# The current-token term of an RWKV layer moved from TensorE to VectorE, with a new written-out order

## The chip, the cores and the metric

One core of one Trainium2 chip. The metric is the device time of one execution, in microseconds (us), a median over several. One execution of each kernel was also taken by the hardware profiler; its rows are the source of every duration below. Engines: PE is TensorE (its weight loads are listed apart as PEld), DVE is VectorE, ACT is ScalarE, POOL is GpSimd, SP is SyncE, which here only issues DMAs.

## The reference

Four batches, eight heads, 768 tokens, head size 48. First an RWKV attention with a decaying state, then a channel MLP on the concatenated heads (384 channels), all in float32:

```python
for t in range(S):                       # attention, per batch and head
    y[t]  = r[t] @ (state + outer(u * k[t], v[t]))
    state = w[:, None] * state + outer(k[t], v[t])

x  = y, heads side by side               # [4, 768, 384]
xn = (x - mean(x)) / sqrt(var(x) + 1e-6) * g_ln
out = x + maximum(xn @ w_ch1, 0) @ w_ch2 # 384 -> 1536 -> 384
```

The part of `y[t]` that uses the token's own key and value is, per head, the scalar `sum_d r[t,d] * u[d] * k[t,d]` times the vector `v[t]`. This is the current-token term.

## The kernel before, in words

**Tiling.** The 3072 tokens are 24 chunks of 128, six chunks per batch. A chunk is a tile of 128 tokens by 384 channels. Step names, which the plan uses, stand in capitals with the chunk number.

**Attention of a chunk.** LK, LR, LV load k, r, v (192 KB each, SP queue). SK and SR multiply k and r by powers of w that depend on the row (tables Fk and Fr), in bfloat16, into `sck` and `scr`. CV casts v into `vv`. TR turns `scr` and `sck` on TensorE into `trs` (TC, or TCr and TCk, copy them out of PSUM); from chunk 14 on TKD turns k, and from chunk 20 on TRD turns r, by DMA instead. AT multiplies the turned tiles, 128 by 128 scores per head; AM (line 365) masks them into `A`. S (lines 382 to 402) adds k^T v into the state's PSUM tile, ZU and ZD turn that into the next state `Z`, Y (lines 428 and 436) gives the attention output from `Z` and `A`. In chunks 1 to 4 (`ZPE`) S also adds the last state into PSUM with one matmul (line 393).

**Current-token term.** Q multiplies the two halves of `trs` element by element (bfloat16, 128x512), on DVE or POOL. In S, four matmuls (line 386) multiply Q by `uwI`, two columns per head pair that hold u*w, so that eight columns of the PSUM tile get the per-head scalars. (r and k carry powers of w whose product leaves 1/w, hence u*w.) CC copies the eight columns out of PSUM into `cc` on ACT or DVE; VB (line 418, POOL) multiplies v by them; X (line 443, DVE) adds this to Y's output.

**MLP.** SQ gives the variance sum, XN the centred activations, RS the scale (POOL). LT and XT turn `xn` on TensorE, or LTD by DMA. UP (line 499) multiplies by the first weight matrix, RL (line 515 or 517) applies the maximum with zero, DN (line 527) multiplies by the second matrix, OT (line 583) scales and adds x, STO stores. `GROUPS` says how many chunks one UP handles, one or two. The first weights come as three blocks of 768 KB (LW1), are multiplied by -g and cast by SW; the second come by three casting DMAs from POOL's queue (IW2).

**Start.** w, as one row, is loaded (WF), its logarithm taken (LN) and spread over 128 rows by one float32 matmul (WBM, line 269); FK and FR make the tables. u and w are also loaded with channels on partitions (ROWSI: four DMAs of 4-byte elements on ACT's queue), as is g (LG, on SP). WL makes the decay of the state `WLZ`, UW makes `uwI`. WU and DU are dummy matmuls on a tile of zeros.

**What sets the order.** Nothing is scheduled at run time. `PLAN` is one list of steps with an engine letter (v, s, g for DVE, ACT, POOL); every engine and DMA queue runs its steps in the order of that list and waits at the head of its own queue. Buffers are rings (`SLOTS`).

Of the kernel before, what the change touches and what calls it, by code (L numbers as in the profile page):

```python
# [13 lines left out]
GROUPS = [1, 1, 1, 1, 1, 1, 1, 1, 2, 2, 2, 2, 2, 2, 1, 1, 1, 1]  # L14
ZPE = [1, 2, 3, 4]
K_BY_DMA = [14, 15, 16, 17, 18, 19, 20, 21, 22, 23]
SLOTS = {'kf': 10, 'rf': 10, 'vf': 10, 'sck': 3, 'scr': 3, 'vv': 4, 'trs': 3, 'q': 2, 'A': 2, 'cc': 4, 'Z': 3, 'ZS': 2, 'Vb': 3, 'x': 13, 'xn': 3, 'xT': 4, 'hT': 4, 'ot': 3}
PLAN = """
MW,0,v WF,0,- TL,0,s MI,0,g WU,13,- MM,0,g MP,0,v LN,0,s LG,0,- ROWSI,0,s WBM,0,- LR,0,-
UGC,0,s FK,0,s LK,0,- FR,0,s LR,1,- SR,0,g WL,0,s SK,0,v LK,1,- UW,0,g DU,24,- TR,0,-  # L20
SR,1,v LK,2,- TCk,0,v SK,1,v LV,0,- TCr,0,v SK,2,v DU,12,- AT,0,- LR,2,- TR,1,- CV,0,s
AMa,0,v LV,1,- Q,0,g AMb,0,v SR,2,v LW1,0,- DU,7,- Y,0,- S,0,- TCk,1,v CC,0,s TCr,1,v
CV,1,s ZU,0,v Q,1,g DU,10,- TR,2,- LV,2,- TC,2,v DU,4,- AT,1,- VB,0,g S,1,- SW,2,s
AMa,1,v LW1,1,- SW,1,g SW,0,s X,0,v Q,2,v CV,2,g XN,0,s AMb,1,v DU,20,- LT,0,- CC,1,v
SQ,0,s Y,1,- ZU,1,v LK,3,- VB,1,g AT,2,- XT,0,v SW,5,s SW,4,v RS,0,g UP,0,- LR,3,-
X,1,v SW,3,s AM,2,v S,2,- SK,3,g XN,1,s LW1,2,- UP,1,- RL,0,s SR,3,v LT,1,- IW2,0,g
SQ,1,s Y,2,- XT,1,v IW2,1,g RL,1,s CC,2,v DU,1,- TR,3,- ZU,2,v VB,2,g UP,17,- LV,3,-
TC,3,s SW,8,g UP,16,- X,2,v RL,17,s SW,7,v IW2,2,g AT,3,- SW,6,v RL,16,s CV,3,g Q,3,v
DU,3,- UP,18,- SQ,2,s XN,2,g UP,2,- AM,3,v RS,2,g RL,18,s LT,2,- DN,0,- RS,1,g XT,2,v
S,3,- RL,2,s UP,34,- CC,3,v VB,3,g Y,3,- RL,34,s ZU,3,v UP,32,- DN,1,- X,3,v UP,33,-  # L30
XN,3,v SQ,3,s LK,4,- RL,32,v LT,3,- DN,2,- RL,33,s XT,3,v RS,3,g LR,6,- UP,48,- SK,4,g
OT,0,v UP,50,- LR,4,- DN,4,- SR,6,v RL,50,s LK,5,- DN,5,- RL,48,s SR,4,v STO,0,- DN,6,-
LK,6,- SK,5,v TR,4,- OT,1,v UP,49,- LR,5,- DN,8,- RL,49,s SK,6,g LV,4,- DN,9,- TC,4,s
SR,5,v DN,10,- LK,10,- Q,4,v TR,5,- CV,4,s OT,2,v AT,4,- LV,5,- TC,5,s S,4,- AM,4,v
DN,12,- LV,7,- CC,4,s TR,6,- VB,4,g ZU,4,v Y,4,- LK,7,- Q,5,v AT,5,- TC,6,s CV,5,g
X,4,v DN,13,- LR,7,- AM,5,v SQ,4,s XN,4,g DN,14,- LV,6,- S,5,- LT,4,- SK,7,v Y,5,-
CC,5,s XT,4,s SR,7,v AT,6,- LR,8,- Q,6,v UP,64,- OT,3,v VB,5,g STO,2,- UP,65,- RL,64,s
AM,6,v LR,9,- TR,7,- RL,65,s UP,66,- LV,10,- X,5,v RS,4,g DN,16,- TC,7,v XN,5,s LK,8,-
SR,8,g DN,17,- SR,9,v RL,66,s CV,6,s LT,5,- LK,9,- AT,7,- SQ,5,s S,6,- Q,7,v DN,18,-
SK,8,g XT,5,s AM,7,v LK,17,- CV,7,s UP,82,- RS,5,g STO,3,- CC,6,s TR,8,- RL,82,s ZU,6,v  # L40
STO,1,- Y,6,- VB,6,g UP,80,- TC,8,v LV,9,- CV,10,s S,7,- X,6,v Q,8,g RL,80,s AT,8,-
LR,14,- XN,6,s Y,7,- OT,4,v UP,81,- CV,9,s SK,9,g AM,8,v LK,11,- DN,20,- RL,81,s SK,10,g
LT,6,- LR,13,- CC,7,v DN,21,- ZU,7,v SQ,6,s XT,6,v VB,7,g DN,22,- LR,10,- UP,96,- ZD,7,g
OT,5,v LV,8,- TR,9,- X,7,v RL,96,s RS,6,g UP,98,- LR,11,- TC,9,v XN,7,s SR,10,g UP,97,-
RL,98,s LR,17,- DN,24,- SQ,7,s Q,9,v SR,11,g CV,8,s LT,7,- STO,4,- AT,9,- XT,7,v RL,97,s
S,8,- LV,13,- TR,10,- UP,112,- SK,11,v CC,8,s TC,10,s LV,11,- ZU,8,v Y,8,- VB,8,g DN,25,-
RL,112,s LR,21,- Q,10,v ZD,8,g UP,114,- X,8,v LK,19,- AM,9,v S,9,- CV,11,g DN,26,- SQ,8,s
LV,14,- TR,11,- XN,8,v CC,9,s OT,6,v VB,9,g Y,9,- TC,11,s LR,12,- AT,10,- ZU,9,v DN,28,-
X,9,v ZD,9,g RL,114,s LK,13,- AM,10,v LT,8,- S,10,- CV,13,s UP,113,- RS,7,g XN,9,s LK,12,-
# [43 lines left out]
def kernel(  # L93
# [170 lines left out]
    def LN(i, e):  # L264
        nc.scalar.activation(out=ln_row[:], in_=w_row[:], func=ACT.Ln)
# [365 lines left out]
```

## Time and profile before

| | us |
|---|---|
| median of six runs | 157.02 |
| lowest and highest of them | 154.81, 158.37 |
| the profiled execution | 155.87 |
| its span in the profile | 154.1 |
| busy: PE, DVE, ACT, POOL | 143.2, 106.2, 88.5, 88.4 |
| MB moved by DMA | 25.53 |

The busy times are shares of one span: PE works during 93% of it, the other engines during 57% to 69%. The granted TensorE clock is 1.00 throughout. Matmul durations of the groups overlap one another, since the ends of matmuls are modelled; how long TensorE really needs for a run of matmuls is read from the chain of work that ended last, or from the distance between starts. So 12 UP matmuls of 128 columns take 0.67 us in an unbroken run, 4 DN matmuls 0.65 us.

### The profile page before, as it was taken

What the parts mean: (1) busy time and instruction counts of PE and PEld (TensorE: products, weight loads), DVE (VectorE), ACT (ScalarE), POOL (GpSimd) and SP (SyncE); (2) the same over time, 40 slices, a digit from 0 to 9 for tenths busy, and PEclk for the clock granted to TensorE, in tenths of its full rate; (3) what the DMA queues carried; (4) which work ended last, traced back from release to release, by engine and by line L of the source; (5) the groups of instructions that cost most, each with busy time, mean ns of one, the idle gap of its engine ahead of it and who ended that gap; (6) DMA issues with size and microseconds to landing.
All of it is one profiled execution on the core that took longest, in us unless ns stands there. A gap on an engine that the chain in (4) does not pass through costs nothing.

```text
span 154.1 us, 4643 instructions
## 1 busy us (share of the span) xinstructions
PE 143.2 (93%) x1866; PEld 115.2 (75%) x1866; DVE 106.2 (69%) x220; ACT 88.5 (57%) x190; POOL 88.4 (57%) x126
## 2 busy tenths in 40 slices
PE   7989597999999999899999999989999999899991
PEld 4877485877786788689678679768787877668880
DVE  2499687655998686978884979895977554555121
ACT  4512895436648658668878559437578345144440
POOL 3535888422575987487931999483734968531100
PEclk9999999999999999999999999999999999999999
DMA  3999899959989899989997989678353663212211
GB/s 50 207 213 359 165 309 208 226 117 216 222 187 240 166 210 203 204 173 197 227 212 146 260 151 220 134 172 152 99 138 79 90 195 98 68 51 78 80 51 51
DMA packets 93142, 25.53 MB, mean 166 GB/s; under 512 B 88385, under 2 KB 91586, under 8 KB 93122
## 3 DMA queue, kind: packets, MB, share of 16 engines
q1 hardware_dynamic: 91858, 24.06, 70.8%
q0 software_dynamic: 432, 1.18, 3.9%
q8 instruction: 14, 0.23, 0.7%
q10 hardware_dynamic: 832, 0.00, 0.3%
q14 instruction: 6, 0.05, 0.1%
HBM read 18.88 MB, written 4.72 MB: 153 GB/s over the span
## 4 chain that ended last, share of the span: by engine, by line
PE 40%; DMA 22%; POOL 10%; DVE 10%; SPq 9%; issue 4%; ACT 2%; DVEq 0%; POOLq 0%
PE o L527 17%; PE hp L499 16%; DMA kf<-in_k_dram 5%; DMA w_sb<-in_moe_w_ch_dram 4%; DMA w_f<-in_moe_w_ch_dram 4%; DVE A L365 4%; DMA xT<-xn 4%; SPq L317 3%; POOL Vb L418 3%; SPq L320 2%; DMA rf<-in_r_dram 2%; SPq L475 2%; POOL sck L201 2%; DMA vf<-in_v_dram 2%; PE at L355 2%
## 5 line engine op out<-in xcount | busy, mean ns | idle before, releaser
L515 ACT ACTIVATE hT<-hp 128x512 bf16<-128x512 f32 x70 | 41.2, 596 | 33.1 <-PE hp L499 32.2
L499 PE MATMUL hp<-xT,w_sb 128*128 128x128 bf16 (+1 forms) x648 | 57.0, 237 | 1.8 <-DMA xT<-xn 1.1
L527 PE MATMUL o<-w_sb,hT 128*128 128x384 bf16 x276 | 53.9, 326 | 1.6 <-DVE ot L583 1.0
L499 PEld LDWEIGHTS <-w_sb 128*128 128x128 bf16 x648 | 48.9, 114 | 6.0 <-DMA xT<-xn 1.6
L527 PEld LDWEIGHTS <-hT 128*128 128x128 bf16 x276 | 24.7, 98 | 13.8 <-issue 1.1
L365 DVE TENSOR_TENSOR A<-at,mask 128x1024 bf16<-128x1024 f32 (+1 forms) x26 | 29.4, 1135 | 0.9 <-PE at L355 0.7
L418 POOL TENSOR_TENSOR Vb<-vf,cc 128x384 f32<-128x384 f32 x24 | 20.2, 841 | 11.8 <-ACT cc L196 7.9
L583 DVE SCALAR_TENSOR_TENSOR ot<-o,rs,x 128x384 f32<-128x384 f32 x23 | 14.1, 614 | 17.0 <-PE o L527 15.7
L450 ACT ACTIVATE sqj<-x,sm 128x384 bf16<-128x384 f32 x24 | 14.7, 612 | 4.4 <-DVE x L443 4.3
L443 DVE SCALAR_TENSOR_TENSOR x<-y,Vb 128x384 f32<-128x384 f32 x24 | 13.3, 552 | 4.3 <-POOL Vb L418 2.8
L201 POOL TENSOR_TENSOR scr<-rf,Fr 128x384 bf16<-128x384 f32 x9 | 9.7, 1081 | 10.0 <-DMA rf<-in_r_dram 6.5
L201 POOL TENSOR_TENSOR sck<-kf,Fk 128x384 bf16<-128x384 f32 x10 | 10.3, 1040 | 8.6 <-DMA kf<-in_k_dram 6.1
L201 POOL TENSOR_TENSOR q<-trs 128x512 bf16<-128x512 bf16 x9 | 10.9, 1208 | 5.9 <-DVE trs L198 3.4
L201 POOL TENSOR_TENSOR Z<-ZS,WLZ 128x384 bf16<-128x384 f32 x12 | 12.2, 1014 | 2.3 <-DVE ZS L412 2.3
L201 DVE TENSOR_TENSOR sck<-kf,Fk 128x384 bf16<-128x384 f32 x14 | 8.6, 619 | 5.6 <-DMA kf<-in_k_dram 5.0
L196 ACT COPY trs<-tr 128x1024 bf16<-128x1024 bf16 (+1 forms) x12 | 10.4, 865 | 3.1 <-PE tr L336 3.1
L467 POOL TENSOR_TENSOR rs<-rs,expo 128x1 f32<-128x1 f32 (+1 forms) x18 | 11.1, 617 | 1.5
L201 DVE TENSOR_TENSOR q<-trs 128x512 bf16<-128x512 bf16 x15 | 8.1, 539 | 4.7 <-ACT trs L196 3.1
L196 ACT CAST vv<-vf 128x384 bf16<-128x384 f32 x16 | 8.2, 510 | 3.9 <-DMA vf<-in_v_dram 1.9
L201 DVE TENSOR_TENSOR scr<-rf,Fr 128x384 bf16<-128x384 f32 x15 | 9.1, 615 | 1.8 <-DMA rf<-in_r_dram 1.7
L259 PE MATMUL o<-warm 128*128 128x128 bf16 x94 | 9.1, 265 | 1.0 <-DVE warm L224 1.0
L355 PE MATMUL at<-trs 48*128 48x128 bf16 x192 | 9.5, 218 | 0.4 <-DVE trs L198 0.2
(72 smaller groups left out, 176.7 us busy)
## 6 DMA issues: line engine op xcount, KB each, us to landing
rf<-in_r_dram SPq DMA_DIRECT2D x24, 192.0 KB, 3.8
kf<-in_k_dram SPq DMA_DIRECT2D x24, 192.0 KB, 4.1
vf<-in_v_dram SPq DMA_DIRECT2D x24, 192.0 KB, 3.8
out_dram<-ot SPq DMA_DIRECT2D x23, 192.0 KB, 2.9
w_f<-in_moe_w_ch_dram SPq DMA_DIRECT2D x3, 768.0 KB, 6.7
w_sb<-in_moe_w_ch_dram POOLq DMA_DIRECT2D x3, 384.0 KB, 7.3
out_dram<-ot SPq DMA_DIRECT2D x2, 96.0 KB, 1.6
trs<-sck SPq DMA_TRANSPOSE x10, 3.0
```

Of the source, the lines that this page charges most:

```text
L196: nc.scalar.copy(out=out, in_=in_)
L201: engines[e].tensor_tensor(out=out, in0=in0, in1=in1, op=ALU.mult)
L355: nc.tensor.matmul(out=t[:, par, q, :], lhsT=trs(i)[p0 : p0 + D, 1, q, :], rhs=trs(i)[p0 : p0 + D, 0, q, :], start=True, stop=True,)
L365: nc.vector.tensor_tensor(out=AA(i)[:, a:b].rearrange("p e q t -> p (e q) t"), in0=psum["at", i][:, a:b].rearrange("p e q t -> p (e q) t") ...
L418: nc.gpsimd.tensor_tensor(out=Vb(i)[:].rearrange("p (h d) -> p h d", h=H), in0=vf(i)[:], in1=cc(i)[:].unsqueeze(2).to_broadcast([P, H, D]) ...
L443: nc.vector.scalar_tensor_tensor(out=xx(i)[:], in0=psum["y", i][:, :C], scalar=1.0, in1=Vb(i)[:], op0=ALU.mult, op1=ALU.add, accum_out=sm[ ...
L450: nc.scalar.activation(out=sqj[:], in_=xx(i)[:], func=ACT.Square, bias=sm[i][:], scale=-float(C), accum_out=sq[g][:, j : j + 1])
L467: nc.gpsimd.tensor_tensor(out=rs[g][:], in0=rs[g][:], in1=expo[:, :n], op=ALU.pow)
L499: nc.tensor.matmul(out=t[:, a * gw : (a + 1) * gw], lhsT=w1_sb[n][kc][:, fb::FB], rhs=xT(g)[:, kc, :gw], start=(kc == 0), stop=(kc == CK - 1),
L515: nc.scalar.activation(out=o, in_=s, func=ACT.Relu)
L527: nc.tensor.matmul(out=psum["o", i][:, :C], lhsT=hT(g)[:, fk, j * P : (j + 1) * P], rhs=w2_sb[d][:, a, :], start=(fk == 0), stop=(fk == FK ...
L583: nc.vector.scalar_tensor_tensor(out=ot(i)[:], in0=psum["o", i][:, :C], scalar=rs[g][:, j : j + 1], in1=xx(i)[:], op0=ALU.mult, op1=ALU.add,)
```

## The change

**The term.** For chunks 8 to 23, Q and the four small matmuls of S fall away. Instead KU multiplies `sck` by a row table `uw_b` (u*w on 128 rows, bfloat16), KR multiplies that by `scr`, and CC becomes a sum over the 48 channels of each head, on DVE. KU runs on DVE for 15 chunks and on POOL for one, KR on DVE for 13 and on POOL for three. The table needs two more loads (LUB, LWB: u and w broadcast to 128 rows) and one product (UWR, POOL). Chunks 0 to 7 keep Q.

**The start.** The DMAs of 4-byte elements are gone. u, w and g are loaded as rows; CL and CU turn ln w, u*w and g into columns with 19 matmuls of one row by one column in float32. UGC, UW and WL read them from PSUM.

**The rest.** `ZPE` is empty: S no longer adds the last state by matmul. `GROUPS` has seven pairs in place of six. Six chunks have r turned by DMA (four before), eight have `xn` turned by DMA (ten before). The whole `PLAN` is another list: the engine of many steps changes, and the order of nearly all of them, the loads at the start among them.

Steps on DVE: Q 15 to 8, SK 14 to 5, SR 15 to 11, XN 8 to 2, SW 3 to 2, CV 3 to 2, XT 8 to 7, TC 4 to 3, RL 2 to 4, copies of CC 10 to 4; new there are 15 KU, 13 KR, 16 sums and the two copies of UW. Steps on POOL: Q 9 to 0, SK 10 to 19, SR 9 to 13, ZD 12 to 16, CV 5 to 7, XN 4 to 0; new are 1 KU, 3 KR, UWR. On ACT: CC 14 to 4, XN 12 to 22, XT 6 to 9, SW 4 to 6. Dummy matmuls: 94 to 103.

```diff
-GROUPS = [1, 1, 1, 1, 1, 1, 1, 1, 2, 2, 2, 2, 2, 2, 1, 1, 1, 1]
-ZPE = [1, 2, 3, 4]
+GROUPS = [1, 1, 1, 1, 1, 1, 2, 2, 2, 2, 2, 2, 2, 1, 1, 1, 1]
+ZPE = []
+CC_BY_DVE = [8, 9, 10, 11, 12, 13, 14, 15, 16, 17, 18, 19, 20, 21, 22, 23]
 PLAN = """
-MW,0,v WF,0,- TL,0,s MI,0,g WU,13,- MM,0,g MP,0,v LN,0,s LG,0,- ROWSI,0,s WBM,0,- LR,0,-
-UGC,0,s FK,0,s LK,0,- FR,0,s LR,1,- SR,0,g WL,0,s SK,0,v LK,1,- UW,0,g DU,24,- TR,0,-
...
+MW,0,v WF,0,- TL,0,s MI,0,g MP,0,v WU,13,- MM,0,g LN,0,s LV,1,- RI,0,s WBM,0,- LW1,1,-
+CV,1,s CL,0,- FR,0,s FK,0,s WL,0,s LR,0,- LK,0,- UR,0,g SR,0,g DU,20,- CU,0,- LK,1,-
+SK,0,v LR,1,- UW,0,v SK,1,v LV,0,- UGC,0,s DU,5,- TR,0,- SW,4,s SW,3,v SR,1,g TCk,0,s
+LK,2,- SW,5,s TCr,0,v LR,3,- Q,0,v DU,16,- AT,0,- SK,2,v TR,1,- LW1,2,- CV,0,g AMa,0,v
+DU,1,- S,0,- AMb,0,v SR,3,g LW1,0,- TCk,1,v DU,14,- Y,0,- CC,0,v TCr,1,v VB,0,g ZU,0,v
+SW,6,s Q,1,v SW,8,g DU,14,- AT,1,- X,0,v S,1,- AMb,1,v XN,0,s IW2,0,g SQ,0,s CC,1,v
+SW,7,v DU,6,- LT,0,- LR,2,- VB,1,g XT,0,v ZU,1,v SW,1,s DU,6,- UP,2,- RS,0,g LV,2,-
+AMa,1,v SW,2,s UP,1,- RL,2,v IW2,1,g SW,0,s LK,3,- Y,1,- SR,2,v IW2,2,g RL,1,s DU,3,-
+TR,2,- CV,2,g X,1,v ZD,1,g TC,2,v DU,5,- UP,0,- XN,1,s SQ,1,s Q,2,v SK,3,g LT,1,-
+AT,2,- XT,1,v LK,4,- S,2,- AM,2,v UP,16,- RL,0,s RS,1,g CC,2,s LV,3,- TR,3,- RL,16,s
+ZU,2,v VB,2,g Y,2,- TC,3,v DN,0,- LR,4,- ZD,2,g X,2,v UP,18,- CV,3,s LK,5,- Q,3,v
...
+    def columns(row, c0):
+        for h in range(H):
+            q, par = divmod(h, 2)
+            nc.tensor.matmul(
+                out=psum["cols"][par * DP : par * DP + D, c0 + q : c0 + q + 1],
+                lhsT=row[0:1, h * D : (h + 1) * D], rhs=ones[0:1, 0:1],
+                start=False, stop=True, skip_group_check=True,
+            )
...
+    def UWR(i, e):
+        times(e, uw_b[:].rearrange("p h d -> p (h d)"), u_b[:], w_b[:])
+
+    def KU(i, e):
+        times(e, ku(i)[:], sck(i)[:, :, :D], uw_b[:])
+
+    def KR(i, e):
+        times(e, kr(i)[:], ku(i)[:], scr(i)[:, :, :D])
...
-        for q in range(HP):
+        for q in range(HP if i not in CC_BY_DVE else 0):
             nc.tensor.matmul(
                 out=t[:, C + 2 * q : C + 2 * q + 2], lhsT=qq(i)[:, q, :], rhs=uwI[:, q, :],
...
     def CC(i, e):
+        if i in CC_BY_DVE:
+            nc.vector.tensor_reduce(out=cc(i)[:], in_=kr(i)[:], axis=mybir.AxisListType.X, op=ALU.add)
+            return
         copy(e, cc(i)[:], psum["s", i][:, C : C + H])
```

## The prediction

> **What bounds the kernel now.** I read the page's busy shares first, then time by stage, the chain of work that ended last, and the waits.
>
> ```profile
> PE 143.2 (93%) x1866; PEld 115.2 (75%) x1866; DVE 106.2 (69%) x220; ACT 88.5 (57%) x190; POOL 88.4 (57%) x126
> ```
>
> TensorE is the busy engine. Time by stage (columns: stretch in us, its length, busy us and instructions of PE, PEld, DVE, ACT, POOL, granted clock, DMA share, GB/s):
>
> ```profile
> 8.00:16.00 8.00, 6.51 (x109) 5.45 (x107) 7.61 (x18) 1.99 (x5) 4.06 (x5) 1.00 1.06 291
> 16.00:24.00 8.00, 6.33 (x116) 5.50 (x117) 6.08 (x15) 7.35 (x16) 6.87 (x11) 1.00 0.99 230
> 28.00:48.00 20.00, 19.98 (x280) 15.57 (x278) 15.74 (x31) 11.31 (x22) 8.22 (x13) 1.00 0.94 192
> 48.00:124.00 76.00, 73.74 (x942) 59.54 (x940) 59.13 (x116) 51.30 (x117) 53.09 (x66) 1.00 0.83 175
> ```
>
> From 28 us on TensorE hardly rests; before, DMA is full and DVE nearly so. The chain (start, us, what) gives what matmuls need in an unbroken run:
>
> ```profile
> 2.11 3.79 DMA kf<-in_k_dram
> ...
> 8.61 6.46 DMA w_f<-in_moe_w_ch_dram
> ...
> 19.57 6.54 DMA w_sb<-in_moe_w_ch_dram
> ...
> 31.28 1.34 PE hp L499 x24
> 32.62 1.95 PE o L527 x12
> 34.57 0.45 PE tr L336 x8
> ...
> 64.20 4.63 DMA kf<-in_k_dram
> ...
> 98.44 2.76 DMA xT<-xn
> ...
> 103.40 0.08 PE s L386 x4
> ...
> 129.61 3.57 DMA xT<-xn
> ```
>
> So 56 ns per UP matmul of 128 columns, 162 per DN, 56 per transpose, 20 to 25 per small s matmul. With these distances all matmuls but the dummies need 128.4 us. At 28.0 us TensorE had done 13.1 us of that (14.9 behind the clock), at 148.0 us 126.0 (22.0 behind). Hence **three terms**: 128.4 of work, 14.9 for the start, 7.1 of stalls later; last, some 4 us of ending, which the change leaves alone. The waits (engine, line, waited for: total, times, longest) say what the stalls hang on:
>
> ```profile
> POOL Vb L418 <- ACT cc L196: 7.9, 6, 2.8
> DVE sck L201 <- DMA kf<-in_k_dram: 5.0, 2, 4.0
> POOL Vb L418 <- DVE cc L198: 3.7, 4, 1.8
> ```
>
> VB waits for CC, thus for Q and TensorE, and X for VB; DVE stands still for a late k. The long transfers at 64, 98 and 130 us in the chain lead to TensorE gaps of 0.8, 0.8 and 0.6 us.
>
> **1. TensorE work.** Gone: 16 chunks x 4 small matmuls x 25 ns = 1.6 us; `ZPE`, 4 x 0.16 = 0.65; two chunks of r by DMA, 8 transposes x 56 ns = 0.45. Added: two LT on TensorE, 6 x 56 ns = 0.34. A pair of chunks in UP costs 0.109 per 256 columns against 2 x 0.056, so about 0.1 less. Sum **-2.5 us**, nearly all on the path that sets the end; covered only where TensorE would have waited.
>
> **2. The start.** The new SP order puts v of chunk 1 and a 768 KB weight block ahead of r and k of chunk 0. At 204 GB/s (4 to 8 us) a chunk's 197 kB takes 0.96 us, at 349 GB/s (12 to 16 us) the block 2.25. First k moves from 5.9 to 5.9 + 3.2 - 0.5 (the load of g, 0.42 to issue, no longer sits ahead) = 8.6; k of chunk 2 comes at 8.6 + 4 x 0.96 = 12.4. DVE stands in order SK2, both halves of AM0, TCk1, CC0, TCr1, ZU0, Q1, X0; with 0.55, 2 x 0.68, 0.42, 0.16, 0.42, 0.55, 0.42, 0.56, each starting some 0.07 before its predecessor's end, X0 ends at 16.4 and, past XN0, LT0, AM1, CC1, SW7 and XT0, the first UP starts near 18.2 (now 17.96, where XN0 waits behind weight casts). Then ZU1, AM1's other half, RL2, SR2, X1, TC2, Q2 and XT1 are 3.9 us of DVE: XT1 ends at 22.1 (now 20.8), and DN0, in order behind Y2 and so behind AM2, starts at 24.0 with 7.6 us of TensorE work done (now 9.8 at that time). In exchange the second weights are issued at 16.3 in place of 19.6 and, with the 6.5 of the row, are there by 22.8 instead of 26.1; today's 0.7 us gap before DN0 goes. Sum **+1.5 us**.
>
> The 19 column matmuls stand ahead of TR0. Between WBM's end (4.3) and TR0 (8.6 + 0.55 = 9.2) 25 dummies at 0.107 take 2.7, which leaves 2.2, or 0.115 each. The trace has no such matmul. The nearest row is WBM: its float32 matmul shows as two records with two weight loads, the second issued 0.165 after the first. Below: 0.05 each, hidden. Above: two loads, 0.33, which makes 6.3 us, 4.1 too many, of which 1.2 is covered by DVE's wait for k of chunk 2. At one load (0.165) it is 0.9 too many, covered. I take **+0.5**, range 0 to 2.9; nothing is gained. What is queued behind: TR0 behind CU on TensorE, SK1 behind UW on DVE, all casts behind UGC on ACT. Start in all: **+2.0** (0 to +6).
>
> **3. DVE.** Rows:
>
> ```profile
> L201 DVE TENSOR_TENSOR q<-trs x15: 410/426/1002, 14.7 to 118.0; 128x512 bf16<-128x512 bf16 x15
> L412 DVE TENSOR_TENSOR ZS<-s,Z 128x384 f32<-128x384 f32 x12 | 6.6, 550 | 0.6 <-ACT cc L196 0.3 <-POOL Z L201 0.2
> ```
>
> The first, with minimum/median/maximum ns, is the nearest to KU and KR: bfloat16, both inputs in SBUF. By size (384 of 512) 0.32 is the low end, 1.0 the high end, I take 0.42. The sum over 48 has no row; low 0.35 (the 384-element copy xT), high 0.62 (OT), taken 0.55 as ZS. Added: 28 x 0.42 + 16 x 0.55 = 20.6. Removed by the moved steps: 9 SK x 0.62, 4 SR x 0.62, 7 Q x 0.54, 6 XN x 0.64, 6 CC x 0.16 and four single casts and copies (2.2), less two RL and two copies of UW (1.7), = 17.2. DVE gains 3.4 over the whole, but about 6 between 48 and 124 us, where SK and Q leave less than KU, KR and sums bring; overlapped, 5.7. There it goes from 59.1 of 76.0 to 64.8 of some 74: 78% to 88%. I charge **+1.0** of new waits (-1 to +5).
>
> The row above spreads from 410 to 1002 ns. The Trainium skill, "SBUF — State Buffer", section "Who interferes with whom", says that a DVE instruction with two SBUF inputs blocks against a GpSimd instruction that reads SBUF, while `tensor_reduce` never does. That speaks against KU and KR: by that rule, if each waited out half a POOL multiply, an estimate from the 1.0 us rows, DVE would get another 14 us and be the bound.
>
> POOL gains about 9 us (10 SK, 4 SR, 4 ZD, 4 KU/KR against 9 Q and 4 XN; 88 to 97), ACT about 5; both stay under 70%. The two broadcast loads are 0.4 MB of 25.5, 2 us of DMA in a stage 90% full, far ahead of KU8: nothing, or 1 us if a load of r or k is pushed.
>
> **4. Later stalls.** Walking both plans with the row durations, I counted how much TensorE work stands between two steps. VB to X, chunks 8 to 23: median 1.3 us before, 8.0 after, as the term no longer needs Q or TensorE. X to the first UP of its group: 5.3 before, 7.2 after. Loads of k to SK, chunks 4 to 8: 1.3 to 2.1 before (a load lands 4.1 after issue), 1.3 to 3.1 after; of r 1.3 to 3.1 and 1.7 to 2.7. SK is on DVE 5 times, not 14, so a late k stops DVE less. Of the 7.1 I take **-3.0** (-5 to 0): the gaps at 64 and 100 and most small ones. What is late next: TRD, whose slack to AT is down to 1.6 (before 4.0 to 9.8), and LTD.
>
> **Sum.** -2.5 + 2.0 + 1.0 - 3.0 = -2.5. The profiled execution took 155.87 (span 154.1), so 153.4 by it. The median of the six is 1.15 above the profiled one: **154.5 us**.
>
> **Rivals.** (a) *Slower: the start.* If a column matmul costs 0.33 and the late first k isn't made up, the start is +6 and the stalls that go are half: 157.0 - 2.5 + 6 + 1 - 1.5 = 160.0. It turns slower than before from a start of +3 on, with -1.5 in stalls. For: DMA full from 4 us, the order of loads. Against: DN0's weights come 3 us earlier. (b) *DVE becomes the bound* from 48 to 124: KU and KR at 0.6 add 28 x 0.18 = 5.0; half of that fits into DVE's idle time, the other half gives back what was saved: 157.0 - 2.5 + 2.0 + 1.0 + 2.5 - 3.0 = 157.0. Against: VB's new slack. (c) *The change gives only its matmuls*: stalls stay, the start is even: 154.5 as well by another way, or with start +2, 156.5.
>
> **Chances.** Forecast 0.50 (its own range 151.5 to 156.0), (a) 0.25, (b) 0.15, (c) 0.10. The range 150.5 to 160.0 leaves out less than a fifth. About 1% (155.45 to 158.6) is what a measurement of this kernel can tell from no change. Faster: most of the forecast and a bit of (c), 0.50; same: 0.22; slower: 0.28.
>
> **What the profile after would show.** Right: no L386 row beyond 32 matmuls; first UP near 18, DN0 near 24; few waits of X for VB and of POOL for cc; KU and KR near 0.42. Wrong: TR0 after 11 us behind column matmuls of 0.3 each; DVE over 90% from 48 to 124 with KU near 0.6; TensorE waiting for `trs` turned by DMA late.

## The result, and the profile after

The median went from 156.89 us (72 runs, 154.01 to 159.59) to 156.22 us (35 runs, 154.53 to 157.95). The ratio after to before is 1.0032 [1.0008, 1.0056]; it is taken over undisturbed runs alone (those at most 1.5% above the fastest of their kernel) and the medians over all, so the two can point different ways. Three later controls (the changed kernel run again, each time beside the kernel before) gave 1.0039 [0.9992, 1.0087], 1.0026 [0.9976, 1.0075] and 1.0092 [1.0056, 1.0128]. So nothing was gained, and perhaps half a per cent lost. The forecast was 154.5.

The profiled execution of the changed kernel took 157.95 us (span 156.0), its longest; the three controls were profiled at spans of 154.1, 154.5 and 153.7. The page, its busy shares and its row of the granted TensorE clock (40 slices, tenths):

```profile
PE 145.5 (93%) x1808; PEld 117.8 (75%) x1808; DVE 112.2 (72%) x230; ACT 92.8 (59%) x190; POOL 97.4 (62%) x133
...
PEclk9999999969999999999999999999999999999999
```

TensorE has 58 matmuls fewer and is busy 2.3 us longer. One slice, at 31 us, has a lower clock; before there was none. Time by stage, columns as in the prediction, the first three rows from one answer and the others from a second:

```profile
8.00:16.00 8.00, 7.46 (x84) 6.76 (x81) 4.61 (x10) 2.10 (x4) 3.25 (x4) 1.00 1.02 243
16.00:24.00 8.00, 7.00 (x127) 6.04 (x128) 7.71 (x21) 6.03 (x12) 6.78 (x11) 1.00 1.02 226
28.00:48.00 20.00, 17.27 (x243) 14.30 (x243) 11.70 (x24) 13.19 (x29) 16.14 (x20) 0.91 0.91 186
...
28.00:36.00 8.00, 5.34 (x74) 4.74 (x73) 3.45 (x8) 4.89 (x11) 5.59 (x6) 0.79 0.86 176
36.00:48.00 12.00, 11.93 (x171) 9.56 (x171) 8.24 (x17) 8.30 (x19) 10.54 (x15) 1.00 0.95 192
48.00:124.00 76.00, 74.12 (x879) 59.15 (x879) 69.33 (x133) 53.41 (x112) 57.34 (x70) 1.00 0.88 179
```

Before, TensorE was busy 19.98 of the 20 us from 28 to 48; now it is 17.27, and all of the loss lies between 28 and 36, where it rests 2.66 us and then runs at a lower clock. After 36 us it hardly rests. The chain of work that ended last, in that place (start, us, what):

```profile
15.56 4.04 SPq L348
...
20.39 10.16 DMA vf<-in_v_dram
...
33.66 1.68 PE hp L553 x24
```

SyncE (SPq, its DMA queue) takes 4.04 us to issue one load of k, and the load of v that it issues at 20.39, that of chunk 3, lands 10.16 us later. The 24 UP matmuls after the gap take 1.68 us; in the chain before, 24 took 1.34. The waits (engine, line, waited for: total, times, longest):

```profile
ACT vv L205 <- DMA vf<-in_v_dram: 6.5, 3, 4.9
POOL Vb L472 <- DVE cc L457: 6.4, 8, 1.7
...
PE s L449 <- ACT vv L205: 2.6, 1, 2.6
```

TensorE (PE) waits in order at the state matmuls S of chunk 3 for `vv`, which ACT casts from that load. From chunk 8 on, VB waits eight times, 6.4 us in all, for the new sum on DVE, where it used to wait for CC behind TensorE. The new operations, minimum/median/maximum ns:

```profile
L210 DVE TENSOR_TENSOR ku<-sck,uw_b x15: 345/790/1168, 50.8 to 118.9; 128x384 bf16<-128x384 bf16 x15
L210 DVE TENSOR_TENSOR kr<-ku,scr x13: 341/361/869, 52.8 to 130.7; 128x384 bf16<-128x384 bf16 x13
...
L457 DVE TENSOR_REDUCE cc<-kr x16: 537/543/553, 54.2 to 131.5; 128x8 f32<-128x384 bf16 x16
```

**Where the time went.** The prediction's measure was the clock time less the unbroken TensorE work done by then; call it the lateness. In us, at five times, for the kernel before and four profiles of the changed kernel (the three last are controls of the experiments):

```
                  24 us   40 us   48 us   124 us   148 us   work in all
before             14.2    15.0    15.7     21.1     22.0      128.4
after              16.6    21.4    21.7     26.0     26.4      125.9
control 1          15.8    20.0    20.4     24.0     24.5      125.9
control 2          16.4    19.9    20.5     24.7     25.0      125.9
control 3          15.5    20.4    20.8     23.8     24.1      125.9
```

The means of the four give: up to 24 us 16.1 - 14.2 = +1.9; from 24 to 40 us 4.3 against 0.8, so +3.5; from 40 to 148 us 4.6 against 7.0, so -2.4; work -2.5. The sum is +0.5 us, and the mean of the four spans is 154.6 us against 154.1. The three controls alone, without the longest execution, give +1.7, +3.4, -2.6 and -2.5, in sum 0.0, and a mean span of 154.1. Before is one profile here, but five runs below share its first 24 us and have 13.8 to 14.2 there; three of them share all to 40 us and have 15.1 or 15.2.

### The profile page after: what moved, and what is told of

Read it like the earlier page. It is cut to its first block, busy times and chain, and to the rows that moved or that the text cites. A ratio compares the mean times of both kernels' runs of the same rounds, so it can differ in the third digit from the quotient of the medians.

```text
span 156.0 us, 4531 instructions
## 1 busy us (share of the span) xinstructions
PE 145.5 (93%) x1808; PEld 117.8 (75%) x1808; DVE 112.2 (72%) x230; ACT 92.8 (59%) x190; POOL 97.4 (62%) x133
## 3 DMA queue, kind: packets, MB, share of 16 engines
q0 software_dynamic: 432, 1.18, 4.2%
## 4 chain that ended last, share of the span: by engine, by line
PE 70%; SPq 12%; DMA 8%; DVE 7%; issue 1%; ACT 0%
PE o L581 27%; PE hp L553 25%; SPq L348 7%; DMA vf<-in_v_dram 7%; PE at L404 4%; PE tr L370 4%; PE y L490 3%; SPq L331 2%; PE s L449 2%; PE y L482 2%; PE tr L538 2%; SPq L351 2%; SPq L354 2%; DMA xT<-xn 2%; DVE ot L637 1%
## 5 line engine op out<-in xcount | busy, mean ns | idle before, releaser
L569 ACT ACTIVATE hT<-hp 128x512 bf16<-128x512 f32 x68 | 39.8, 595 | 29.7 <-PE hp L553 28.9
L472 POOL TENSOR_TENSOR Vb<-vf,cc 128x384 f32<-128x384 f32 x24 | 21.8, 907 | 9.8 <-DVE cc L457 6.4
L210 POOL TENSOR_TENSOR sck<-kf,Fk 128x384 bf16<-128x384 f32 x19 | 20.0, 1057 | 6.7 <-DMA kf<-in_k_dram 6.1
L210 POOL TENSOR_TENSOR scr<-rf,Fr 128x384 bf16<-128x384 f32 x13 | 13.4, 1033 | 7.9 <-DMA rf<-in_r_dram 6.7
L210 POOL TENSOR_TENSOR Z<-ZS,WLZ 128x384 bf16<-128x384 f32 x16 | 16.3, 1017 | 1.5 <-DVE ZS L466 1.0
L510 ACT ACTIVATE xn<-x,sm 128x384 bf16<-128x384 f32 x22 | 13.5, 613 | 2.1 <-DVE x L497 2.0
L210 DVE TENSOR_TENSOR ku<-sck,uw_b 128x384 bf16<-128x384 bf16 x15 | 10.8, 725 | 1.7 <-POOL sck L210 1.7
L518 POOL TENSOR_SCALAR rs<-sq 128x1 f32<-128x1 f32 (+1 forms) x17 | 3.4, 202 | 10.6 <-ACT sqj L504 9.6
L210 DVE TENSOR_TENSOR sck<-kf,Fk 128x384 bf16<-128x384 f32 x5 | 3.5, 708 | 8.7 <-DMA kf<-in_k_dram 8.7
L490 PE MATMUL y<-vv,A 128*128 128x48 bf16 x192 | 9.0, 185 | 0.8 <-DVE A L414 0.8
```

Of the source, the lines that this page charges most:

```text
L210: engines[e].tensor_tensor(out=out, in0=in0, in1=in1, op=ALU.mult)
L472: nc.gpsimd.tensor_tensor(out=Vb(i)[:].rearrange("p (h d) -> p h d", h=H), in0=vf(i)[:], in1=cc(i)[:].unsqueeze(2).to_broadcast([P, H, D]) ...
L490: nc.tensor.matmul(out=t[:, h * D : (h + 1) * D], lhsT=AA(i)[:, par, q, :], rhs=vv(i)[:, h, :], start=first, stop=True, skip_group_check=True,
L510: nc.scalar.activation(out=xn(i)[:], in_=xx(i)[:], func=ACT.Identity, bias=sm[i][:], scale=-float(C))
L569: nc.scalar.activation(out=o, in_=s, func=ACT.Relu)
```

## The experiments

The first four ran on one chip without the changed kernel as control, and the kernel before had a median of 158.79 there, 2 to 4 us more than elsewhere. The changed kernel's own ratio on that chip is not known, and the medians of w2_late and r0_first there (156.87, 156.36) are those of the changed kernel elsewhere (156.0 to 156.4). So what these four say is read from their profiles, and their ratios below 1 are not taken as a gain. In the plan's code, "-" and "+" lines are stretches of the list. Medians (lowest to highest), ratio to the kernel before on the same chip, lateness:

```
run            median us               ratio [95%]               24 us  40 us  148 us
w2_late        156.87 (154.44-158.95)  0.9794 [0.9710, 0.9878]    16.0   20.3   25.4
r0_first       156.36 (155.81-158.21)  0.9865 [0.9816, 0.9915]    15.6   19.8   24.6
no_ku          156.10 (154.64-159.60)  0.9811 [0.9746, 0.9876]    15.6   19.8   23.3
term_only      162.94 (161.44-163.52)  1.0258 [1.0194, 1.0322]    13.9   15.2   31.1
after_again    156.02 (154.53-160.20)  1.0039 [0.9992, 1.0087]    15.8   20.0   24.5
v3_early       159.42 (154.82-160.06)  -                          15.9   24.3   28.4
keep_clock     156.26 (154.69-156.76)  1.0039 [0.9998, 1.0080]    16.6   20.8   24.9
start_v3       157.35 (154.95-161.51)  1.0077 [1.0021, 1.0133]    15.5   24.2   28.3
after_third    156.37 (154.69-158.08)  1.0026 [0.9976, 1.0075]    16.4   19.9   25.0
w2_split       157.59 (155.46-158.81)  1.0098 [1.0043, 1.0154]    17.0   22.7   26.3
best           157.18 (156.62-157.96)  1.0137 [1.0078, 1.0196]    15.8   22.0   25.8
best_v3        156.52 (155.13-157.61)  1.0072 [1.0025, 1.0118]    15.3   19.9   25.0
after_fourth   156.42 (155.32-157.51)  1.0092 [1.0056, 1.0128]    15.5   20.4   24.1
old_start2     158.79 (157.65-159.06)  1.0220 [1.0173, 1.0267]    13.8   21.0   25.5
old_start3     160.31 (158.20-160.89)  1.0279 [1.0214, 1.0345]    14.2   16.7   29.0
old_start4     162.63 (162.32-163.24)  1.0490 [1.0442, 1.0537]    13.8   15.1   30.4
after_no_w2    153.71 (152.77-154.32)  0.9872 [0.9826, 0.9919]    15.5   17.9   22.1
before_no_w2   154.80 (153.95-155.79)  0.9949 [0.9912, 0.9986]    13.8   15.2   21.1
```

### The parts one by one

**w2_late**: the second weight's casting loads of blocks 1 and 2 later on POOL's queue.

```diff
-RL,2,v IW2,1,g SW,0,s
+RL,2,v SW,0,s
...
-SR,2,v IW2,2,g RL,1,s
+SR,2,v RL,1,s
...
-SK,3,g LT,1,-
+SK,3,g IW2,1,g LT,1,-
...
-SK,4,g AT,3,-
+SK,4,g IW2,2,g AT,3,-
```

> The changed kernel with one edit: the casting loads of the second and third block of the second weights (IW2,1 and IW2,2) are issued from POOL's queue after SK3 and after SK4 instead of right behind RS0; no arithmetic changes. Theory A (the start gives the gain back: these two loads, needed by TensorE only at 35 and 42 us, take the DMA engines while v of chunk 3 is under way, which lands at 30.6, 10 us after its issue, and TensorE stands for 2.75 us and then runs at a lower clock until 36 us): v of chunk 3 lands before 26 us, the gap at 28.4 us goes, and the kernel is 2 to 4 us faster than the changed kernel, that is 1 to 2.5% below the kernel before. Rival B (DVE is the bound between 48 and 124 us, whatever comes before is waited for there): v lands early, but the time stays within 0.5% of the changed kernel, since DVE, 91% busy there, takes up the gain. Rival C (the transfers are limited by bytes, and holding two of them back only moves the late ones): another load is late, TensorE stands by the same 2 to 3 us at DN1 or SK4.

Measured: v of chunk 3, issued at 19.45, lands by 25.9 us and the gap before S of chunk 3 is gone. TensorE is 16.6 us late at 28 us but 20.3 at 40: three new gaps of 0.5, 0.5 and 1.1 us follow between 27.7 and 30.7, the last for `scr` of chunk 4, which POOL multiplies late, behind SK of chunk 4 (1.18 us) and the issue of a casting load (0.62 us). Time by stage:

```profile
28.00:36.00 8.00, 6.44 (x84) 5.54 (x85) 4.46 (x8) 5.42 (x13) 7.28 (x9) 0.79 1.12 229
```

POOL is busy 7.28 of the 8 us here. The late v is caused by the casting loads, but with v in time POOL is what is late next, and the lateness at 40 us is that of the controls. None of the three forecasts is met whole: A's early v came without A's gain, B puts the loss behind 48 us, and C expects another late load.

**r0_first**: r and k of chunk 0 first on SP's queue, chunk 0 turned ahead of the u columns, eight dummies in place of 20.

```diff
-LN,0,s LV,1,- RI,0,s WBM,0,- LW1,1,- CV,1,s CL,0,-
+LN,0,s RI,0,s WBM,0,- CL,0,-
...
-SR,0,g DU,20,- CU,0,- LK,1,-
+SR,0,g DU,8,- LK,1,-
...
-TR,0,- SW,4,s SW,3,v SR,1,g TCk,0,s LK,2,- SW,5,s TCr,0,v
+TR,0,- CU,0,- SR,1,g TCk,0,s UGC,0,s LK,2,- LV,1,- LW1,1,- TCr,0,v UW,0,v
```

> The changed kernel with the loads at the start put as before the change: r and k of chunk 0, then k1, r1, v0, k2 ahead of v of chunk 1 and the first weight block; to match, CV1 and the weight casts SW3 to SW5 come later in their queues, the column matmuls of u and g come behind TR0, and 12 of the 20 dummies ahead of them go. The second weights stay as in the changed kernel. Theory A (the start costs what the sum said, 1.5 us for the late first k): first k lands near 5.5 instead of 8.9 us, the first UP starts 1 to 2 us earlier than 19.75, TensorE is 1 to 2 us less behind at 28 us; but v of chunk 3 is still late, so the time falls by 0 to 1.5 us only. Rival (DVE sets the start, not the loads): the first UP stays within 0.5 us of 19.75 and the time does not change.

Measured: k of chunk 0 comes 3.5 us earlier (its SK starts at 5.45 us in place of 9.01). Yet the first UP, at 18.71 us, is within the 18.4 to 19.8 of the changed kernel's four profiles, so an earlier first k brings no earlier UP. v of chunk 3 still lands 10.1 us after its issue, the gap before S is 2.1 us, and TensorE is 19.8 us late at 40 us, next to the controls' 19.9 to 20.4.

**no_ku**: KU left out, so that the term of chunks 8 to 23 lacks the factor u*w.

```diff
-        times(e, kr(i)[:], ku(i)[:], scr(i)[:, :, :D])
+        times(e, kr(i)[:], sck(i)[:, :, :D], scr(i)[:, :, :D])
```

> The changed kernel without KU in chunks 8 to 23: KR multiplies sck by scr directly, so u*w is left out of the current-token term of these chunks. It takes 15 DVE instructions of 0.73 us and one of POOL away, 11 us of DVE time, in the stage where DVE is 91% busy. Theory A (DVE is not the bound; the gaps at 84 and 90 us are all that it costs): 0 to 1.5 us faster than the changed kernel. Rival B (DVE is the bound there): 3 us faster or more, and DVE's busy share between 48 and 124 us falls while TensorE's rises by about as many us as are saved.

Measured, time by stage:

```profile
48.00:124.00 76.00, 75.54 (x898) 60.21 (x898) 62.95 (x122) 53.00 (x109) 57.78 (x71) 1.00 0.86 179
```

DVE falls to 62.95 us of 76, from 69.3 to 71.0 in the four profiles of the changed kernel. From 40 to 148 us 3.5 us are lost, against 3.7 to 5.1 there. So by this one profile KU costs between 0.2 and 1.6 us: DVE, busy for 91% to 93% of the stage, is not its bound, as theory A had it.

**term_only**: the kernel before with its own plan, in which only the term of chunks 8 to 23 is moved (KU, KR and the sum, all on DVE; one more `scr` buffer).

```diff
+        LUB=LUB, LWB=LWB, UWR=UWR, KU=KU, KR=KR,
...
-Q,8,g
+KU,8,v KR,8,v
...
-CC,8,s
+CC,8,v
```

> The kernel before, with the old order and the old start, and only the term of chunks 8 to 23 moved: KU, KR and the sum, all on DVE, where Q stood and where CC stood; the table uw_b is added and the ring of scr has four buffers in place of three. 64 small matmuls go (1.6 us), DVE gets 16 KU, 16 KR and 16 sums (28 us by the changed kernel's durations of 0.73, 0.47 and 0.54) for 10 Q and 6 copies (6 us), POOL loses 6 Q (7 us). Theory A (the term's move pays only with an order that makes room on DVE): slower than before by 2 to 6 us, DVE waits named in TensorE's gaps. Rival (DVE has the room anyway, and TensorE is the bound): faster by 1 to 1.6 us.

Measured: 162.94 us, 2.6% slower than before, although TensorE has less to do. At 40 us it is as early as before (15.2), then it loses 15.9 us up to 148 us:

```profile
48.00:124.00 76.00, 70.89 (x851) 55.82 (x849) 68.33 (x139) 48.78 (x103) 44.24 (x56) 0.98 0.82 174
```

DVE is busy 68.33 us, TensorE only 70.89, POOL 44.24. Put where Q and CC stood, the moved term does not fit the old order; other places for it in that order were not tried. In the changed kernel DVE is as busy, but POOL takes 57.34 us, and 4.6 us are lost in place of 15.9. That new order has its price earlier.

### Is it one late load?

**after_again**: the changed kernel as control. In this expectation the ratio is read the wrong way round: 1.0032 is after over before.

> The changed kernel as it is, beside the kernel before on the chip of the next three runs, so that their times can be set against it. The measured ratio so far is 0.997 (1.0032 as before over after). All theories expect the same here: 0.99 to 1.005 of the kernel before, TensorE 21 to 22 us behind its unbroken work at 40 us, a gap of 2.1 to 2.8 us before the state matmuls of chunk 3, and a granted clock of 0.7 to 0.9 between 28 and 36 us.

Measured: gap and ratio as expected; TensorE is 20.0 us late at 40 us, 1 us less than expected, and the clock stayed at 1.00 between 28 and 36 us behind the gap of 2.56 us. From 24 to 40 us it still loses 4.2 us, against 4.8 in the first profile, so by these two profiles the clock is worth less than a microsecond.

**v3_early**: one load moved.

```diff
-LV,2,- AMa,1,v
+LV,2,- LV,3,- AMa,1,v
...
-CC,2,s LV,3,- TR,3,-
+CC,2,s TR,3,-
```

> One DMA issue is moved: v of chunk 3 goes right behind v of chunk 2 on SyncE's queue, ahead of two loads of k, so it is issued near 15.6 us and not 20.4 us, before the second part of the second weight is called for at 20.9 us. Theory (the 4.4 us lost between 28 and 36 us are v of chunk 3 held back by the casting weight loads, and the lower clock after the gap): v lands by 25 us, the gap before the state matmuls of chunk 3 is under 0.5 us, the clock between 28 and 36 us is at least 0.9, TensorE is 17.5 to 18.5 us behind at 40 us, and the time is 2.5 to 3.5 us below the changed kernel. Rival (the DMA engines are the limit in this stage, and whatever is held back is waited for): k or r of chunk 3 or 4 lands as late as v did, another gap of 1.5 to 2.5 us takes the place of this one, the clock drops as before, and the time is within 1 us of the changed kernel.

Measured: the rival's late k, with more lost than it says. Five of the six executions took 158.7 to 160.1 us; the sixth took 154.82, and no profile shows why. The profile is of one of the five. The chain of work, then the waits:

```profile
15.46 3.42 SPq L344
...
18.92 10.09 DMA kf<-in_k_dram
```

```profile
POOL sck L200 <- DMA kf<-in_k_dram: 6.3, 1, 6.3
```

v takes the place on SP's queue that k had, its issue takes 3.4 us, k of chunk 3 is issued at 18.92 and lands 10.09 us later. It is needed earlier than v, and TensorE now stands for 5.8 us. In nine of the runs in which the casting loads stay where they were, the input on which chunk 3 or 4 then hangs (v, k or r) was issued between 18.2 and 20.4 us and lands at 28.5 to 30.9. Not every load issued there is so late: in r0_first k of chunk 4, issued at 18.27, lands 5.54 us later.

**keep_clock**: 40 dummy matmuls ahead of S of chunk 3.

```diff
         t = psum["s", i] = ps.tile([P, 512], FP32, name="s")
+        for _ in range(40 if i == 3 else 0):
+            nc.tensor.matmul(out=t[:, :P], lhsT=warm[:], rhs=warm[:], start=True, stop=True)
```

> The late v stays; 40 matmuls of constants (0.056 us each, 2.2 us) are put ahead of the state matmuls of chunk 3, into the gap in which TensorE waits for v. Theory (the gap lowers the granted clock, and 24 UP matmuls at 1.7 to 1.9 us for a group of six and not 1.34 cost 1.5 us or more): clock at least 0.95 between 28 and 36 us, UP groups back at 1.34, 1.0 to 1.6 us below the changed kernel, with the 2.7 us of the wait itself still lost. Rival (the clock falls for another reason, or what it costs is hidden behind the next waits, on VectorE above all): the clock or the time does not move, within 0.4 us of the changed kernel.

Measured: the granted clock of all twelve executions is 0.996 or more over the span, where five of the control's twelve reached that and the others had 0.978 to 0.989. The clock does fall because of the gap. The median does not move (156.26 against 156.02). The longest execution falls from 160.20 to 156.76. The forecast gain of 1.0 to 1.6 us is not there.

**start_v3**: r0_first and v3_early together.

> The start in the order of the run in which r and k of chunk 0 are loaded ahead of v of chunk 1 and the first weight's block 1, and chunk 0 is turned ahead of the u columns; and v of chunk 3 as in the run with that load moved. Theory (the start and the late v are two separate losses that add): first UP near 18.7 us, 16 to 17.5 us behind at 40 us, 3.5 to 4.5 us below the changed kernel, the fastest of all. Rival (both only move waiting about before one bound in 28 to 48 us, the DMA engines): no more than 0.7 us below the better of the two alone.

Measured: 157.35 us, k of chunk 3 issued at 18.18 and landing 10.28 us later, 24.2 us late at 40 us. The profile is of a long execution, 159.98; the shortest of the twelve took 154.95. The theory of two losses that add falls.

### Loads off the path, and what then is late

**after_third**, the control:

> The changed kernel once more as the control of this chip. All theories: 0.99 to 1.01 of the kernel before, v of chunk 3 landing 9 to 11 us after its issue, a gap of 2.1 to 2.8 us before the state matmuls of chunk 3, TensorE 19.8 to 21.5 us behind at 40 us.

Measured: 156.37 us; here the wait is shared, 1.26 us for k and 1.20 us for v of chunk 3, and the lateness at 40 us is the same, 19.9.

**w2_split**: as w2_late, with `IW2,2` behind `SK,5`.

> The casting loads of the second weight's blocks 1 and 2 wait behind the decayed keys of chunks 3 and 5 on GpSimd's queue (issued near 25 and 32 us in place of 20.9; they are wanted near 35 and 42 us). Theory (loads that SyncE issues from about 19 us on stand behind these casting blocks and land 10 us later): v of chunk 3 lands by 26 us, the gap before its state matmuls is gone, no gap over 0.6 us from 24 to 40 us because GpSimd's queue is free for r of chunk 4 where the earlier run with these loads late had it held, 17.5 to 18.5 us behind at 40 us, 2.0 to 3.0 us below the changed kernel on this chip. Rival (the DMA engines or the weight itself are the limit, so what is put off is waited for later): the second weight's block 1 or 2 or an input of chunk 4 or 5 is late, 1 us or more is lost between 30 and 48 us, and the time is within 0.7 us of the changed kernel.

**best**: r0_first and w2_split together.

> The late casting loads of the run before and the start in which r and k of chunk 0 come first and the u columns are turned behind chunk 0. Theory (two separate losses): first UP near 18.7 us, 16.5 to 17.5 us behind at 40 us, 3.0 to 4.0 us below the changed kernel and below the kernel before. Rival (one bound, the DMA engines from 8 to 30 us, behind both): no more than 0.5 us below the run with the casting loads alone.

**best_v3**: best, and `LV,3` ahead of `LK,4`.

> As the run before, and v of chunk 3 issued ahead of k of chunk 4. Theory: with the casting loads out of the way the order of these two decides nothing, so within 0.5 us of the run before. Rival (the place on SyncE's queue decides, as in the run with v of chunk 3 moved): k of chunk 4 lands after 29 us, a gap of 1 us or more before the turning of chunk 4, 1 us or more above the run before.

Measured: 157.59, 157.18 and 156.52 us, none below the control. In best and best_v3 the loads were in time, and at 32 us TensorE was 17.6 and 17.1 us late, 1.5 to 3 us earlier than the four profiles of the changed kernel (19.1 to 20.1). In w2_split TensorE still waited 1.4 us for `sck` of chunk 3. Then a new gap of 2.8 and 2.6 us opened, 2.2 in w2_split, each time at the turning of `xn`. No late input is behind it. The timeline of best_v3 (start, us, engine, line, operation):

```profile
30.41 0.62 POOL L335 DMA_DIRECT2D w_sb<-in_moe_w_ch_dram  x1
...
30.88 3.23 DVE L200 TENSOR_TENSOR q<-trs 128x512 bf16<-128x512 bf16 x1 [1.71 <-ACT trs L195]
...
31.07 0.84 POOL L462 TENSOR_TENSOR Vb<-vf,cc 128x384 f32<-128x384 f32 x1
...
31.86 1.01 POOL L200 TENSOR_TENSOR Z<-ZS,WLZ 128x384 bf16<-128x384 f32 x1
...
32.82 0.99 POOL L200 TENSOR_TENSOR scr<-rf,Fr 128x384 bf16<-128x384 f32 x1
...
34.03 0.54 DVE L487 SCALAR_TENSOR_TENSOR x<-y,Vb 128x384 f32<-128x384 f32 x1
...
34.62 0.61 ACT L500 ACTIVATE xn<-x,sm 128x384 bf16<-128x384 f32 x1 [2.78 <-DVE x L487]
```

A Q that took 0.41 us elsewhere takes 3.23, from the issue of the casting load through three POOL multiplications without a break, and ends 0.3 us after the third. X stands behind it on DVE, and XN behind X. It is 3.50 us in best and 2.83 in w2_split, where Q began 0.23 us after the issue had ended. No DVE multiplication of the other profiles takes more than 1.5 us. The row of POOL steps alone is not the cause: the changed kernel has it too. In after_third the same three run without a break, and Q, issued during the first, takes 0.43 us:

```profile
32.85 0.84 POOL L472 TENSOR_TENSOR Vb<-vf,cc 128x384 f32<-128x384 f32 x1
...
33.57 0.43 DVE L210 TENSOR_TENSOR q<-trs 128x512 bf16<-128x512 bf16 x1 [0.77 <-ACT trs L205]
33.65 1.21 POOL L210 TENSOR_TENSOR Z<-ZS,WLZ 128x384 bf16<-128x384 f32 x1
...
34.81 1.01 POOL L210 TENSOR_TENSOR scr<-rf,Fr 128x384 bf16<-128x384 f32 x1
```

There it is Z that gets longer, 1.21 us in place of 1.01. New in the three runs is the casting load that POOL issues right before the three steps (`IW2,2`, which the edit moved there), so this gap comes with the edit. How that load's issue holds Q so long is not shown, and another place for it was not tried.

### Is it the order, or the load on the DMA engines?

Three runs keep the order of the kernel before (with its start and its columns brought by DMA) up to one of its steps, and then take the steps that are left in the changed kernel's order: old_start2 up to `RL,18`, old_start3 up to `DN,10`, old_start4 up to `DN,18`.

**after_fourth**, the control:

> The changed kernel as control of this chip. All theories: 0.99 to 1.01 of the kernel before, one input of chunk 3 late by 1 to 3 us, TensorE 19.5 to 21.5 us behind at 40 us and 4 to 5 us more at 148 us.

Measured: 156.42 us, the gap before S of chunk 3 is 2.36 us, v issued at 18.70 and landing 10.23 us later.

> The start of the kernel before (its order and its columns brought by DMA) up to its step RL,18, which it reaches near 26 us, and from there the changed kernel's order, without what is done. Theory (what is lost from 24 to 40 us is that the new order asks for chunks 3 to 5 there, while in the old one TensorE works on the feed-forward part of chunks 0 to 3 and the inputs have time to land): the new order asks for chunk 4 right behind chunk 3 here too, so an input of chunk 4 or 5 is late, a gap of 1.5 to 3 us between 27 and 36 us, 17.5 to 19.5 us behind at 40 us. Rival (only the changed start, its loads and columns, costs the time): no gap over 0.6 us, 15 to 16 us behind at 40 us, the same as in the next run.

Measured: with the old start, 13.8 us late at 24 us as before, TensorE stands 4.2 us for r of chunk 4, issued at 18.69 and landing 12.19 us later; 21.0 us late at 40 us. Gap and lateness are larger than the theory said, but in its direction: the changed start is not the cause of the loss from 24 to 40 us, since the new order meets it from the old start too.

> The same with the order of the kernel before up to its step DN,10, near 37.6 us, so with the feed-forward part of chunks 0 to 2 and a part of 3 ahead of chunk 4. Theory: no gap over 0.6 us from 24 to 40 us, 15 to 16.5 us behind at 40 us, 4 to 6 us more up to 148 us as in the changed kernel, so the 2.5 us of the matmuls and the 2 us of later waits are kept: a span of 150 to 152.5 us, 2 to 4 us below the changed kernel and below the kernel before. Rival (the early order pays for the later one: the changed order needs chunks 4 to 6 turned early, or VectorE, at 91% busy, has nothing in hand): the 4 us come back as waits between 40 and 124 us, and the time is within 1 us of the changed kernel.

> The same with the order of the kernel before up to its step DN,18, near 49 us. Theory: as the run before within 1 us (the start ends before 38 us). Rival (chunks held back early cost VectorE's cover later): more waits between 50 and 124 us than in the run before, 1 to 4 us above it.

Measured: 16.7 and 15.1 us late at 40 us, near what the theory had, and then 12.3 and 15.3 us more up to 148 us, in place of 4 to 6. The forecast span of 150 to 152.5 is missed (159.0 and 160.6); as the rival said, the gain comes back as waits, and more than that. It is lost at the seam: 8.6 us between 40 and 64 us in old_start3 and 10 us between 48 and 64 in old_start4. In old_start4 POOL stood there for the row of u, which the splice asks for as soon as it is loaded:

```profile
POOL uw_b L198 <- DMA u_b<-in_u_dram: 6.5, 1, 6.5
```

After 64 us they lose 3.7 and 4.5 us, the control 2.8. The two say that the orders do not join well like this; whether a better joint would keep both gains stays open.

**after_no_w2** and **before_no_w2**: the casting loads of blocks 1 and 2 left out of both kernels, zeros in their place.

```diff
         nc.vector.memset(expo[:], -0.5)
+        for n in (1, 2):
+            nc.vector.memset(w2_sb[n][:], 0.0)
...
     def IW2(n, e):
-        nc.gpsimd.dma_start(out=w2_sb[n][:], in_=w2_src[:, n])
+        if n == 0:
+            nc.gpsimd.dma_start(out=w2_sb[n][:], in_=w2_src[:, n])
```

> The changed kernel without the casting loads of blocks 1 and 2 of the second weight; zeros stand in their place, so two thirds of the second product are left out of the result, while every matmul still runs. Theory (in the changed order the wait for inputs of chunks 3 to 5 is a matter of what the DMA engines must move before 30 us): no input of chunks 3 to 5 is late, no gap over 0.6 us from 24 to 40 us, 16.5 to 18 us behind at 40 us, 2.5 to 4 us below the changed kernel (some 152.5 to 154). Rival (the new order itself, one chunk's chain after another with no feed-forward work between, makes TensorE wait): still over 19.5 us behind at 40 us, within 1 us of the changed kernel.

> The same two loads left out of the kernel before, zeros in their place. Theory (its order gives the inputs of chunk 4 the time up to 38 us, so the fill of the DMA engines costs it little): the gap of 0.7 us before its first feed-forward product stays, since that waits for block 0, 14.5 to 15.2 us behind at 40 us, within 1 us of the kernel before. So without these loads the changed kernel is faster than the kernel before by 1 to 3 us, the forecast's 2.5 among these. Rival: the kernel before gains as much as the changed one, 2 us or more, and the order of the two stays as it is.

Measured: 153.71 and 154.80 us; the changed kernel gains 1.5 to 2.2% against the ratios of its controls, which ran on other chips, the kernel before 0.5%. Time by stage of the changed kernel without these loads:

```profile
24.00:28.00 4.00, 3.85 (x69) 3.23 (x67) 3.32 (x7) 2.49 (x5) 3.83 (x7) 1.00 0.98 197
28.00:36.00 8.00, 7.01 (x122) 6.14 (x123) 5.60 (x12) 5.87 (x14) 7.08 (x11) 1.00 0.95 197
```

and of the kernel before without them:

```profile
28.00:36.00 8.00, 8.00 (x111) 6.61 (x109) 5.05 (x11) 3.13 (x7) 2.45 (x5) 1.00 0.40 85
```

The DMA share of the kernel before drops from 0.84 to 0.40 in this stage and its lateness does not change (15.2 at 40 us), as the theory had it. It has no use for these bytes here: it works on the MLP of chunks 0 to 3. The changed kernel is 17.9 us late at 40 us in place of 19.9 to 21.4. With these loads out it is the faster of the two, by a ratio of 0.9872/0.9949 = 0.992, half of the 1.6% that was forecast. What is left of the early loss, 2.4 us from 24 to 40 against 1.4 in before_no_w2, is mostly three waits of 0.4 to 0.6 us for DVE and ACT.

## Why the prediction was wrong, by its steps

**TensorE work, -2.5: right.** 128.4 to 125.9 us in every profile.

**The start, +2.0: right in size.** The prediction counted it up to 28.0 us. There the four profiles are 16.9 us late in the mean (16.5 to 17.7) and the kernel before 14.9, so +2.0; up to 24 us they have +1.3 to +2.4. In detail it was less exact: the first UP came at 18.4 to 19.8 us (18.2 forecast) and DN0 at 24.6 to 26.8 (24.0). The columns, booked with +0.5, end at 9.5 us in the first profile, and TR of chunk 0 starts at 9.98 behind five dummies; those of 48 columns took about 0.08 us each, those of 128 columns 0.43.

**Later stalls, -3.0, with DVE's +1.0 a net -2.0: wrong. This is the step that failed.** From 28 to 148 us the kernel before loses 7.1 us and the four profiles 8.1, so +1.0 in place of -2.0, and these 3 us are the whole miss. What was forecast did come, but only behind 40 us: from 40 to 148 us they lose 3.7 to 5.1 us, before 7.0, and in the first profile X waits 0.6 us for VB in place of 2.8. VB's wait for `cc` got smaller there, not small (9.0 us in place of 11.6), and is now for DVE. What was not booked is a new wait ahead of that, for the inputs of chunk 3. The step weighed the loads of k and r for chunks 4 to 8 with "a load lands 4.1 after issue"; chunk 3 and v are not in it. The new order asks for chunks 3 and 4 there; the old one works on the MLP and asks for chunk 4 only later. In the four profiles v of chunk 3, issued between 18.7 and 20.4 us, landed 10.0 to 10.5 us later, beside the casting loads. From 24 to 40 us that made 3.5 us more than before. The trace of before had shown such landings, in its DMA issues from 8 to 36 us (KB each, median us to landing) and, for r, as minimum, median and maximum:

```profile
vf<-in_v_dram SPq DMA_DIRECT2D x5, 192.0 KB, 3.9
...
rf<-in_r_dram SPq DMA_DIRECT2D x4, 192.0 KB, 8.4
```

```profile
DMA to landing us min/median/max: 3.6/8.4/12.0
```

There v of chunk 3, issued at 17.74, lands in 5.3 us, and the r issued at 18.90, that of chunk 6, in 12.0, but its SR runs only at about 32 us. One landing time for all loads was the error. The forecast also booked the second weight as a pure gain of the start. The gap before DN0 did go, but blocks 1 and 2 of it are what held back chunk 3 (w2_late, after_no_w2).

**DVE, +1.0: the price not contradicted, the durations wrong.** DVE came to 69.3 to 71.0 us of 76 between 48 and 124, 91% to 93%, in place of 64.8 of 74. The sum cost 0.544 (0.55 forecast), KR 0.469 and KU 0.725 (0.42 each). Five KU that began while POOL stood still took 0.345 to 0.353 us, ten that began while POOL computed took 0.350 to 1.168, median 0.97. That fits the rule which the prediction quoted from the Trainium skill, "SBUF — State Buffer", section "Who interferes with whom", and did not book: two SBUF inputs on DVE against a reading GpSimd. Its other half fits as well, `tensor_reduce` spreads by 16 ns alone. The estimate of 14 us from it was too high: KU and KR took 15 x 0.305 + 13 x 0.049 = 5.2 us more than booked. By no_ku all of KU costs 0.2 to 1.6 us of time.

**The rivals.** (a) named the start as the place, and that the balance turns from a start of +3 on: up to 40 us it is +5.4, and the kernel did not get faster. Its cause was wrong: r0_first, with the columns later and the first k earlier, is as late at 40 us. (b)'s signs came, DVE over 90% and KU above 0.6, but the loss from 48 to 124 us is less than before. (c) had the stalls stay as they were. In sum they nearly do, and its 156.5 is near the median of 156.22, but that is luck: the stalls behind 40 us shrank, and a new one ahead of them took their place.

**Shown and not shown.** Shown: the place of the loss (24 to 40 us), that without the casting loads 2 us of it or more are gone, and that the old order does not have it. Not shown: that an order exists with both the old one's early stage and the new one's later one. No run with the whole computation in it and the changed kernel beside it as control was faster than the kernel before.

## What to carry to other kernels

A forecast of a new order needs a landing time for every load from the moment it is issued, not one mean: in the kernel before, a load issued at 17.74 us landed in 5.3 us, and one issued at 18.90 in 12.0. When a step is moved to another engine, take its duration from rows in which the other engines work as they will then: KU took 0.345 us while POOL stood still and up to 1.17 while it worked. A wait that is taken away in a stage where DMA, POOL and DVE are all nearly full shows the next one, so price the stage and not the wait.

## What the runs showed that I had not expected

A DVE multiplication with both inputs in SBUF, 0.41 us long elsewhere, became 2.83, 3.23 and 3.50 us long behind the issue of a casting load and three POOL multiplications. The Trainium skill, "SBUF — State Buffer", section "Summary: rules for kernel authors", has the second one to issue block until the first finishes. That fits after_third, where Q got in between two POOL steps; in the three long cases Q waited for three steps in a row, and why is open.

The clock fell after some short rests of TensorE and not after others of the same length: not after 2.56 us (after_again) and 2.47 (no_ku), but after 2.75 (after), 2.36 (after_fourth) and 2.13 (r0_first), to 0.79 on the mean of 28 to 36 us. In w2_late it fell as far with three rests of 0.5, 0.5 and 1.1 us. Dummy matmuls in the gap kept it up in all twelve executions of keep_clock.
